# Moving one group of value loads two head pairs later in the source of a fused attention and maxout kernel

## The chip, the cores and the metric

The kernel runs on one core of a Trainium2 chip. The metric is the device time of one execution in microseconds (us). The time before is 335.61 us, the median of five executions that lie between 333.82 and 337.74 us.

## What is computed

The first half is attention with a relative position bias, for 8 batches, 8 heads, 576 positions and 64 values per head; the second is a feed-forward layer with three parallel products and an elementwise maximum. Cut to what matters:

```
scores = q @ k^T / 8 + bias_table[bucket(|i - j|)]      # per batch and head, 576 x 576
attn   = exp(scores - max) / sum(exp(scores - max))
x      = (attn @ v), heads side by side                 # 4608 tokens x 512
h      = maximum(maximum(x @ w1, x @ w2), x @ w3)       # 4608 x 768
out    = h @ w_out                                      # 4608 x 512
```

The inputs are float32; the kernel turns them into bf16 as it loads them, and multiplies in bf16.

## The kernel before

**Batches and head pairs.** After a first batch with a code of its own, one loop runs over batches b = 1 to 7 and, within each, over head pairs hp = 0 to 3 (two heads of 64 fill the 128 partitions). A head pair has two halves. Each half begins with a visit (`visit`): TensorE multiplies kT and qT into PSUM (`sc`), ScalarE takes the exponential (L479) into a tile `e`. VectorE multiplies in the bias band (L473). Then comes an `attend` (tile `a`), the product of such exponentials with the values.

**Late products.** `attend` isn't called at once. Each head pair puts two calls, one per half, in the list `late`, and each half of the loop takes one out (`next_late`). So the values of batch 2 are first read one head pair after batch 2 has begun: batch 2, head pair 0 still multiplies the values of batch 1, head pair 3.

**Feed-forward work as filling.** The products with the weights (`ps`, `pso`) of the batch before are cut into portions, and `fill` puts some of them between the attention products of each half, so that TensorE has work while ScalarE takes exponentials.

**Loads.** `load_q`, `load_k` and `load_v` each issue DMAs from POOL's queue that read float32 from HBM and write bf16 to SBUF. For a whole batch, `load_v` issues four DMAs of 128 KB (as written) into `vx` (L134), one per 128 positions, and two of 32 KB into `vt` (L151) for the last 64 positions: six in all, 576 KB. There are two `vx` and two `vt` buffers; batch b uses number b modulo 2. So batch 2's values overwrite batch 0's, and may be written only when the last `attend` of batch 0 has been done. That one is taken out of `late` in batch 1, head pair 0, second half.

**Crossbar transposes.** The matrix products need q and k with the head dimension on the partitions. For batch 0 and 1, TensorE transposes them. From batch 2 on, DMA transposes do (`transposes`, L415), ten per batch, issued from SP's queue: for each of five groups of positions one for q and one for k. Those of batch 2 are called for in batch 1, one group per half; the generator `crossbar` holds what is left of them. Their sources are the tiles `q_sb` and `k_sb`, which the loads write.

**What sets the order.** Work that is passed through `inorder` (`keep_in_program_order`) stays in the order of the source on its engine. The loads aren't passed through it: the scheduler of the tile framework places them on POOL's queue by their dependences and their place in the source. On the chip each engine then runs its own queue in order, and waits on semaphores for what it needs from others.

**Where the loads of batch 2 and 3 are called.** `load_q` and `load_k` of batch 2 are called in batch 0, last head pair; `load_v` of batch 2 in batch 1, head pair 0, at the end of the second half, after the `attend` and the portions were chosen, as it is for each later batch in the batch before it; `load_q` and `load_k` of batch 3 in batch 1, head pair 3. Between those calls, no other code gives POOL work.

Of the kernel before, what the change touches and what calls it, by code (L numbers as in the profile page):

```python
# [39 lines left out]
def kernel(  # L40
# [13 lines left out]
    B, H, S, D = q.shape  # L54
# [98 lines left out]
    def load_q(b, h0, h1):  # L153
        load_main(q, b, h0, h1, batch[b][0])
        load_tail(q, b, h0, h1, q_diag)

    def load_k(b, h0, h1):
        load_main(k, b, h0, h1, batch[b][1])
        load_tail(k, b, h0, h1, k_diag)

    def load_v(b, h0, h1):
        load_main(v, b, h0, h1, vx[b % 2][:, :, :, 0:D])
        load_tail(v, b, h0, h1, v_diag)
# [14 lines left out]
    def load_tiles():  # L178
        q_sb = loads.tile([P, KT, H, D], BF16, tag="q_sb", name="q_sb")
        k_sb = loads.tile([P, KT, H, D], BF16, tag="k_sb", name="k_sb")  # L180
        return q_sb, k_sb
# [189 lines left out]
    def store_outputs():  # L371

        while stores:
            stores.pop(0)()

    def add_ffn(t0, nt, last=False):
        portions, left = ffn(t0, nt, last)
        portions[0] = rest + portions[0]
        rest[:] = left
        pending.extend((sum(n for n, _ in p), [fn for _, fn in p]) for p in portions)  # L380

    def early():

        if pending and None in pending[0][1]:
            n, fns = pending[0]
            i = fns.index(None)
            for fn in fns[:i]:
                fn()
            pending[0] = (n, fns[i + 1 :])

    def fill(target, *hooks):

        groups, spent, hooks = [], 0, list(hooks)
        while pending and (not groups or spent + pending[0][0] <= target):
            n, fns = pending.pop(0)
            spent += n
            groups += [fn for fn in fns if fn]
        for j, group in enumerate(groups):
            while hooks and (j == len(groups) - 1 or j > 0 and len(hooks) > len(groups) - 1 - j):
                hooks.pop(0)()  # L400
            group()
        for hook in hooks:
            hook()


    def transposes(b):

        made = qk_tiles()
        qk.append(made)

        def one(j, t):
            src = batch[b][j][:, t].rearrange("p h d -> p (h d)") if t < KT else (
                (qtail, ktail)[j][b % 2][:].rearrange("p h c -> p (h c)")
            )
            inorder(nc.sync.dma_start_transpose(out=made[j][:, :, P * t : P * t + P], in_=src))  # L415

        for t in range(KT + 1):
            one(0, t)
            one(1, t)
            yield  # L420
# [37 lines left out]
    def second_transposes(made, hp):  # L458

        hs = slice(2 * hp, 2 * hp + 2)  # L460
        tp = ps_s.tile([P, 2, 2 * CH], BF16, tag="sc", name="tp")
        for j, tl in enumerate((qtail, ktail)):
            for t in range(KT):
                tr(tp[:, j, P * t : P * t + P], batch[1][j][:, t, hs, :].rearrange("p h d -> p (h d)"), ident[:])
            tr(tp[:, j, KT * P : KT * P + P], tl[1][:, hp, :], ident[:])
        for j in range(2):
            dve_copy(made[j][:, hp, :], tp[:, j, 0 : (KT + 1) * P])

    def times_band(hp, e4, t, lo, hi, put=lambda x: x):
        lo, hi = max(lo, P * t - P), min(hi, P * t + 2 * P)  # L470
        if lo < hi:
            c0, c1 = BAND - (hi - P * t + P), BAND - (lo - P * t + P)
            put(nc.vector.tensor_tensor(  # L473
                out=e4[:, t, :, lo:hi], in0=e4[:, t, :, lo:hi],
                in1=hank[:, 2 * hp : 2 * hp + 2, c0:c1][:, :, ::-1], op=ALU.mult,
            ))
# [4 lines left out]
    def visit(qT, kT, e4, c, mid=None):  # L481


        for tt in range(0, KT, 2):
            sc = ps_s.tile([P, 2, 2, QS], F32, tag="sc", name="sc")
            for t in range(2):
                for par in range(2):
                    r = slice(64 * par, 64 * par + 64)
                    mm(
                        sc[:, par, t, :], lhsT=kT[r, P * (tt + t) : P * (tt + t) + P],  # L490
                        rhs=qT[r, c * QS : c * QS + QS],
                    )
            exp(e4[:, tt : tt + 2, :, c * QS : c * QS + QS].rearrange("p t h q -> p h t q"), sc[:])
            if tt == 0 and mid:
                mid()

    def left_keys(hp, qT, kT, el, lo, hi, sc=None):


        if sc is None:  # L500
            sc = ps_s.tile([P, 2 * CH], F32, tag="sc", name="sct")
        for q0 in range(lo, hi, CH):
            q1 = min(q0 + CH, hi)
            mm(sc[:, q0 - lo : q1 - lo], lhsT=kT[:, KT * P :], rhs=qT[:, q0:q1])
        exp(el[:, lo:hi], sc[:, 0 : hi - lo])


    def times_bandt(hp, el):
        inorder(nc.vector.tensor_tensor(
            out=el[:, S - 192 : S + 64], in0=el[:, S - 192 : S + 64], in1=bandt[:, hp, :], op=ALU.mult  # L510
        ))

    def left_queries(hp, qT, kT, el):

        sc = ps_s.tile([P, KT, 2 * 64], F32, tag="sc", name="scq")
        for t in range(KT):
            mm(sc[:, t, :], lhsT=kT[:, P * t : P * t + P], rhs=qT[:, QM : QM + P])
        eq = el[:, S + 64 :].rearrange("p (t h q) -> p t h q", t=KT, h=2)
        exp(eq, sc[:].rearrange("p t (h q) -> p t h q", h=2))
# [68 lines left out]
    def x_tile():  # L588
        return xs.tile([P, KT + 1, d_model], BF16, tag="x_sb", name="x_sb")
# [3 lines left out]
    def next_late():  # L593
        return late.pop(0)() if late else (lambda: None)

    def e_tiles():
        return (
            ep.tile([P, KT, 2, QM], BF16, tag="e4", name="e4"),
            ep.tile([P, S + 64 + KT * P], BF16, tag="el", name="el"),
        )  # L600
# [62 lines left out]
    for hp in range(HP):  # L663
# [18 lines left out]
        def queries():  # L682
            left_queries(hp, qT, kT, el)
            times_band_left(hp, el)
# [28 lines left out]
    for b, hp in [(b, hp) for b in range(1, B) for hp in range(HP)]:  # L713
        if hp == 0:
            x_sb[b] = x_tile()
        qT, kT = (x[:, hp, :] for x in qk[b])
        e4, el = e_tiles()
        rate = 8 if b == 1 or (b, hp) == (2, 0) else 13

        visit(qT, kT, e4, 0)
        store_outputs()
        if b == 1:
            if hp == 0:
                crossbar = transposes(2)
            next(crossbar, None)
        elif hp and b + 1 < B:
            if hp == 1:
                crossbar = transposes(b + 1)  # L730
            next(crossbar)
        early()
        if turned:
            turned.pop(0)()
        quotients = next_late()
        times_band(hp, e4, 0, 0, QS, inorder)
        quotients()
        fill(rate, lambda: left_keys(hp, qT, kT, el, 0, S + 64))
        times_bandt(hp, el)


        visit(qT, kT, e4, 1)
        store_outputs()
        if b == 1 or hp in (1, 2) and b + 1 < B:
            next(crossbar, None)
        early()
        if turned:
            turned.pop(0)()
        quotients = next_late()
        times_band(hp, e4, 1, 0, QM, inorder)  # L750
        quotients()
        if b == 1 and hp + 1 < HP:
            second_transposes(qk[1], hp + 1)
        if hp == 1:
            add_ffn((b - 1) * CH if b > 1 else QS, CH if b > 1 else QS)
        if hp == 0 and b + 1 < B:
            load_v(b + 1, 0, H)
        if hp == (HP - 1 if b == 1 else 0) and b + 2 < B:
            batch[b + 2] = load_tiles()
            load_q(b + 2, 0, H)  # L760
            load_k(b + 2, 0, H)

        def queries():
            left_queries(hp, qT, kT, el)
            times_band(hp, e4, 3, 0, QM, inorder)

        fill(rate, lambda: times_band(hp, e4, 2, 0, QM, inorder), queries)
        times_band_left(hp, el)
        for half in range(2):
            late.append(lambda b=b, hp=hp, e4=e4, el=el, half=half: attend(b, hp, e4, el, half))  # L770
# [44 lines left out]
```

## Time and profile before

| what | value |
|---|---|
| median of five executions | 335.61 us (333.82 to 337.74) |
| the profiled execution | 337.74 us |
| its span, first to last instruction | 336.0 us |
| TensorE (PE) busy | 312.4 us, 93% of the span |
| VectorE (DVE) busy | 212.7 us, 63% |
| ScalarE (ACT) busy | 201.3 us, 60% |
| GpSimd (POOL) busy | 118.4 us, 35%, nearly all of it issuing DMAs |
| moved by DMA | 40.65 MB, 121 GB/s on average |
| mean granted TensorE clock | 0.985 |

The span lies 1.74 us below the time of the same execution. Times in the views are microseconds from the first instruction. "SPq" and "POOLq" are the queues of those engines, where the issue of a DMA takes its time; the landing of the data comes later. A tail in square brackets says how long the engine sat idle before the instruction, and what ended that.

### The profile page before, as it was taken

Reading aid. Unit: us, or ns where it says so; the run is one execution under the profiler, and the core shown is the slowest. Engines: PE = TensorE matmul, PEld = TensorE weight load, DVE = VectorE, ACT = ScalarE, POOL = GpSimd, SP = SyncE. Lnnn points to the kernel's source line nnn. Section 1 sums busy time; section 2 is a strip of 40 time slices with the busy share of each in tenths; the row PEclk is TensorE's granted clock in tenths of the full one; section 3 lists DMA queues with packets and bytes.
Section 4 is the critical chain, followed back from the end, with each engine's and each line's share of the span. In section 5 each row is a group of like instructions: output and inputs, shape, how many; then the busy total and the mean of one; then the engine's idle time right before and its main releaser. Section 6 shows DMA issues by size and latency. Waiting matters only on the chain.

```text
span 336.0 us, 7932 instructions
## 1 busy us (share of the span) xinstructions
PE 312.4 (93%) x3183; PEld 177.2 (53%) x3224; DVE 212.7 (63%) x526; ACT 201.3 (60%) x270; POOL 118.4 (35%) x157
## 2 busy tenths in 40 slices
PE   6878879929999999999999999999999999999995
PEld 2346657717655555555555555555555554444442
DVE  6386667724766676667666766677667666444452
ACT  3699767735877766776677667766776661021221
POOL 8932994609874760294096000410000000000000
PEclk9999999966999999999999999999999999999999
DMA  9999999999999999999999960496022103301103
GB/s 159 150 213 179 99 139 134 121 176 150 141 185 158 150 135 198 137 141 170 234 114 110 174 176 13 58 164 189 19 49 86 64 2 66 132 1 62 64 0 125
DMA packets 171781, 40.65 MB, mean 121 GB/s; under 512 B 163672, under 2 KB 167264, under 8 KB 171744
## 3 DMA queue, kind: packets, MB, share of 16 engines
q0 software_dynamic: 110688, 16.72, 80.2%
q1 hardware_dynamic: 59840, 23.02, 37.2%
q8 instruction: 25, 0.41, 0.5%
q10 hardware_dynamic: 1216, 0.40, 0.5%
q14 instruction: 12, 0.10, 0.1%
HBM read 35.39 MB, written 9.45 MB: 133 GB/s over the span
## 4 chain that ended last, share of the span: by engine, by line
PE 75%; DMA 12%; POOL 8%; issue 2%; SPq 2%; DVE 1%; ACT 0%; POOLq 0%; DVEq 0%
PE ps L94 38%; PE a L94 13%; PE pso L94 12%; PE sc L94 8%; DMA w_bf<-in_moe_w_dram 5%; DMA wo_bf<-in_moe_w_out_dram 3%; PE sct L94 2%; POOL q_sb L134 2%; POOL vx L134 2%; SPq L415 2%; DMA k_sb<-in_k_dram 2%; PE scq L94 2%; DMA kT<-k_sb 2%; POOL k_sb L134 1%; POOL vt L151 1%
## 5 line engine op out<-in xcount | busy, mean ns | idle before, releaser
L94 PE MATMUL ps<-xT,w_bf 128*128 128x512 bf16 (+1 forms) x692 | 154.2, 360 | 1.5
L479 ACT ACTIVATE e<-sc 128x1024 bf16<-128x1024 f32 x128 | 124.9, 1024 | 36.7 <-PE sc L94 36.6
L94 PEld LDWEIGHTS <-w_bf 128*128 128x128 bf16 x720 | 66.4, 99 | 57.6 <-issue 1.7
L473 DVE TENSOR_TENSOR e<-e,hank 128x512 bf16<-128x512 bf16 (+2 forms) x136 | 59.8, 467 | 31.3 <-ACT e L479 29.7
L299 ACT ACTIVATE m<-ps 128x512 bf16<-128x512 f32 x54 | 32.3, 598 | 67.1 <-PE ps L94 64.8
L318 DVE TENSOR_TENSOR m<-ps,m 128x512 bf16<-128x512 f32 x54 | 37.3, 691 | 47.5 <-ACT el L479 27.1
L94 PEld LDWEIGHTS <-kT 64*128 64x128 bf16 (+1 forms) x704 | 36.2, 96 | 47.7 <-issue 27.1
L94 PE MATMUL pso<-wo_bf,hT 128*128 128x512 bf16 x203 | 50.5, 379 | 1.2 <-DVE hT L323 0.5
L94 PE MATMUL sc<-qT,kT 64*128 64x256 bf16 x512 | 42.6, 280 | 9.6 <-DMA kT<-k_sb 4.4
L94 PE MATMUL a<-vx,e 128*128 128x65 bf16 x1024 | 45.5, 194 | 0.0
L134 POOL DMA_DIRECT2D q_sb<-in_q_dram x32 | 28.2, 906 | 38.7 <-DMA kT<-k_sb 25.2
L94 PEld LDWEIGHTS <-e 128*128 128x128 bf16 x1024 | 41.2, 98 | 0.9
L323 DVE TENSOR_TENSOR hT<-ps,m 128x512 bf16<-128x512 f32 x54 | 37.0, 686 | 6.3 <-PE ps L94 4.6
L94 PE MATMUL a<-vt,el 128*128 128x130 bf16 (+1 forms) x192 | 39.9, 214 | 0.9 <-DMA vt<-in_v_dram 0.9
L564 DVE TENSOR_TENSOR x_sb<-a,rd 128x256 bf16<-128x256 f32 (+1 forms) x64 | 31.4, 491 | 2.2
L110 DVE COPY osb<-pso 128x512 f32<-128x512 f32 (+1 forms) x33 | 22.6, 684 | 13.9 <-PE pso L94 10.5
L94 PEld LDWEIGHTS <-hT 128*128 128x128 bf16 x216 | 19.6, 98 | 21.8 <-DVE hT L323 1.5
L94 PEld LDWEIGHTS <-el 128*128 128x128 bf16 x448 | 24.1, 97 | 12.4 <-issue 10.1
L134 POOL DMA_DIRECT2D vx<-in_v_dram x32 | 28.7, 927 | 3.9 <-DMA k_sb<-in_k_dram 1.9
L134 POOL DMA_DIRECT2D k_sb<-in_k_dram x28 | 24.7, 908 | 5.2 <-DMA wo_bf<-in_moe_w_out_dram 4.3
L479 ACT ACTIVATE el<-sct 128x640 bf16<-128x640 f32 (+2 forms) x36 | 23.1, 644 | 3.3 <-PE sct L94 2.6
L479 ACT ACTIVATE el<-scq 128x512 bf16<-128x512 f32 x32 | 19.1, 597 | 8.8 <-PE scq L94 8.7
(61 smaller groups left out, 163.0 us busy)
## 6 DMA issues: line engine op xcount, KB each, us to landing
out_dram<-osb SPq DMA_DIRECT2D x35, 256.0 KB, 2.7
vx<-in_v_dram POOLq DMA_DIRECT2D x32, 128.0 KB, 7.0
q_sb<-in_q_dram POOLq DMA_DIRECT2D x26, 128.0 KB, 5.9
k_sb<-in_k_dram POOLq DMA_DIRECT2D x24, 128.0 KB, 6.2
w_bf<-in_moe_w_dram POOLq DMA_DIRECT2D x3, 768.0 KB, 14.3
xT<-in_k_dram SPq DMA_DIRECT2D x6, 128.0 KB, 4.4
hank<-w_dr SPq DMA_DIRECT2D x2, 384.0 KB, 7.1
wo_bf<-in_moe_w_out_dram POOLq DMA_DIRECT2D x1, 768.0 KB, 10.6
```

Of the source, the lines that this page charges most:

```text
L94: inorder(nc.tensor.matmul(*args, **kw))
L110: inorder(nc.vector.tensor_copy(out_, in_))
L134: nc.gpsimd.dma_start(out=dst[:, t, h0:h1, :], in_=x[:, t, h0:h1, :])
L151: nc.gpsimd.dma_start(out=dst(b, par, h0, h1), in_=tail_part(src, b, h0, h1, par))
L299: nc.scalar.activation(out=st[fb]["m0"][:], in_=st[fb]["ps0"], func=ACTF.Copy)
L318: inorder(nc.vector.tensor_tensor(out=m[:], in0=st[fb]["ps1"], in1=st[fb]["m0"][:], op=ALU.max))
L323: inorder(nc.vector.tensor_tensor(out=hT[:, fb * CH : fb * CH + CH], in0=ps2, in1=st[fb]["m"][:], op=ALU.max))
L415: inorder(nc.sync.dma_start_transpose(out=made[j][:, :, P * t : P * t + P], in_=src))
L473: put(nc.vector.tensor_tensor(out=e4[:, t, :, lo:hi], in0=e4[:, t, :, lo:hi], in1=hank[:, 2 * hp : 2 * hp + 2, c0:c1][:, :, ::-1], op=ALU. ...
L479: nc.scalar.activation(out=out_, in_=in_, func=ACTF.Exp, scale=inv_sqrt_d)
L564: inorder(nc.vector.tensor_tensor(out=x_sb[b][:, 2 * half : 2 * half + n, P * hp : P * hp + P].rearrange("p t (h d) -> p t h d", d=D), in0 ...
```

## The change

The call of `load_v` that stands in batch 1 moves from head pair 0 to head pair 2. It loads the values of batch 2, the third batch. In each later batch the call stays at head pair 0.

```
         if hp == 1:
             add_ffn((b - 1) * CH if b > 1 else QS, CH if b > 1 else QS)
-        if hp == 0 and b + 1 < B:
+        if hp == (2 if b == 1 else 0) and b + 1 < B:
             load_v(b + 1, 0, H)
         if hp == (HP - 1 if b == 1 else 0) and b + 2 < B:
             batch[b + 2] = load_tiles()
             load_q(b + 2, 0, H)
             load_k(b + 2, 0, H)
```

In the source the call stood behind the calls for two of the five groups of batch 2's transposes; it then stands behind all five. It still stands ahead of the loads of batch 3's q and k.

More of the change, by code (lines that the diff above doesn't have):

```diff
@@ L755 @@
             add_ffn((b - 1) * CH if b > 1 else QS, CH if b > 1 else QS)
-        if hp == 0 and b + 1 < B:
+        if hp == (2 if b == 1 else 0) and b + 1 < B:
             load_v(b + 1, 0, H)
```

## The prediction

> **What bounds the kernel now.** I read the page's shares and its chain first, then the waits of TensorE, then the timelines of POOL, SP and TensorE around the change (40 to 90 us), then the order in which the two built programs' instructions stand on each engine.
>
> The page, part 1 and part 4:
>
> ```profile
> PE 312.4 (93%) x3183; PEld 177.2 (53%) x3224; DVE 212.7 (63%) x526; ACT 201.3 (60%) x270; POOL 118.4 (35%) x157
> ...
> PE 75%; DMA 12%; POOL 8%; issue 2%; SPq 2%; DVE 1%; ACT 0%; POOLq 0%; DVEq 0%
> ```
>
> TensorE is busy for 93% of the span, and 75% of the chain that ended last. So a DMA matters only where TensorE waits for it. TensorE's waits between 50 and 110 us are these (engine, line, what it waited for, us in total, times, longest):
>
> ```profile
> PE sc L94 <- DMA kT<-k_sb: 4.4, 3, 2.1
> PE sc L94 <- DMA qT<-q_sb: 1.7, 1, 1.7
> PE sct L94 <- ACT e L479: 0.2, 1, 0.2
> ```
>
> No row has the values (`vx`, `vt`) as its cause; the first two are the transposes. They fall at one place, the beginning of batch 2. TensorE's timeline there (start, us, instruction, count, idle before):
>
> ```profile
> 59.05 0.22 PE L97 MATMUL tp<-ident,ktail 128*128 128x128 bf16 x1
> ...
> 69.31 0.28 PE L94 MATMUL sc<-qT,kT 64*128 64x256 bf16 x2 [1.68 <-DMA qT<-q_sb]
> 70.82 0.39 PE L94 MATMUL sc<-qT,kT 64*128 64x256 bf16 x2 [1.23 <-DMA kT<-k_sb]
> 72.27 0.40 PE L94 MATMUL sc<-qT,kT 64*128 64x256 bf16 x2 [1.05 <-DMA kT<-k_sb]
> 74.77 0.40 PE L94 MATMUL sc<-qT,kT 64*128 64x256 bf16 x2 [2.10 <-DMA kT<-k_sb]
> ...
> 83.78 0.41 PE L94 MATMUL a<-vx,e 128*128 128x65 bf16 x8
> ```
>
> The four holes are 1.68 + 1.23 + 1.05 + 2.10 = 6.06 us. The first row is the last instruction of the transposes by TensorE that the source calls in batch 1, head pair 2 (`second_transposes`); I use it below as a clock for the place in the source. The last row is the first product with batch 2's values: visit and `attend` in batch 2, head pair 1. Batch 2, head pair 0 multiplies batch 1's (its `attend`s are those at 75.18 and 81.07).
>
> POOL's timeline shows when the moved loads are really issued:
>
> ```profile
> 55.69 2.64 POOL L134 DMA_DIRECT2D k_sb<-in_k_dram  x3 [4.29 <-DMA wo_bf<-in_moe_w_out_dram]
> 58.30 1.33 POOL L151 DMA_DIRECT2D ktail<-in_k_dram  x2
> 59.62 3.54 POOL L134 DMA_DIRECT2D vx<-in_v_dram  x4
> 63.73 1.26 POOL L151 DMA_DIRECT2D vt<-in_v_dram  x2 [0.58 <-DMA k_sb<-in_k_dram]
> 74.82 3.53 POOL L134 DMA_DIRECT2D q_sb<-in_q_dram  x4 [9.83 <-issue]
> ```
>
> **The change, part by part.** It removes no instruction and adds none; it moves six DMA issues in the source. What matters is where they stood on POOL's queue, and what they waited for.
>
> *What the old place was worth.* The old call stands behind the last `attend` of batch 0, whose products TensorE finishes at about 41.7 us (the row `a<-vx,el` at 41.55, four products, 0.28 us). If POOL had been free, the values could have been issued then. They were issued at 59.62, 17.9 us later, because twelve loads of q and k of batch 2 stand ahead of them, the last of which ends at 58.30 + 1.33 = 59.63. POOL went from that row to the values without a gap. So nothing in the old place decided their time: POOL's queue did.
>
> *What the new place asks for.* It stands behind batch 1, head pair 2's `second_transposes`, whose last instruction starts at 59.05 on TensorE, 0.57 us ahead of 59.62. Even if the scheduler tied the loads to the place in the source, TensorE's order would ask POOL to wait for nothing: it would be past that place. But POOL has no such tie. It waits on semaphores alone: for a free DMA lane and for TensorE's last reading of the buffer (at 41.7 us), neither of which the move touches.
>
> *Which queue neighbours they pass.* None. Between the two places the source gives POOL nothing else to do: ahead of the six stand the q and k loads called in batch 0, and behind them those of batch 3, called in head pair 3. On SP, the transposes and the stores stay where they are, since they are another queue's. The built programs say the same. In both, POOL's rows around the six are (row, line, instruction, semaphores waited for):
>
> ```
> 60 L151 DMACopy ktail_99<-in_k_dram 64x4x64 [waits DMASW3_49]
> 61 L151 DMACopy ktail_99<-in_k_dram 64x4x64 [waits DMASW4_49]
> 62 L134 DMACopy vx_93<-in_v_dram 128x8x64 [waits DMASW5_49,PE_49]
> ...
> 67 L151 DMACopy vt_95<-in_v_dram 64x4x64 [waits DMASW2_49]
> 68 L134 DMACopy q_sb<-in_q_dram 128x8x64 [waits DMAHW5_49,DMAHW3_49,DMAHW7_49,DMAHW1_49,DMASW3_49]
> ```
>
> All 160 rows of POOL and 139 of SP are the same. On TensorE, VectorE and ScalarE the rows differ in the serial numbers within tiles' names (`ps_875` becomes `ps_869`: six loads fewer were named ahead of it), and in nothing else. With those numbers left out, the two programs agree in every instruction, buffer address, semaphore and waited-for value. The move is visible in the source and not on the chip.
>
> *The sum.* Issue of the six: 4 x 0.9 + 2 x 0.64 = 4.9 us before (rows of 3.54 us for four and 1.26 us for two), 4.9 us after, at the same place: 0. TensorE's holes before batch 2: 6.06 us before and after: 0. Waits added: none, so nothing is queued behind one. The cover of the loads stays too: the last `vt` issue starts at about 64.4 and its kind lands within 7.6 us (the range in this window is 7.3 to 7.6), so at 72.0; first need at 83.7, that is 11.7 us to spare. There is no cost that the trace leaves unknown, hence nothing to bound. The profiled execution stays at 337.74 + 0 = 337.74 us (336.0 span and 1.74 outside it). That execution is the slowest of the five, 2.13 us above their median, and nothing in the change prefers it, so the forecast for the median is **335.6 us**.
>
> The Trainium skill has a rule against such a move: "DMA: Bandwidth & Descriptors", section "Rules for kernel authors", tells authors to issue a DMA early and wait late, so that its fixed cost is overlapped. By it a later issue loses cover, and the sum would be above 335.6. The rows decide: the issue is at 59.62 by the queue, whichever place the source names.
>
> **The rivals.**
>
> *Faster: the loads do move behind the transposes.* The transposes of batch 2 run from 56.33 (first issue on SP) to 74.7, and the loads are issued among them; in the stretches from 60 to 75 us DMA moves 113, 157 and 159 GB/s. The six write 4 x 128 + 2 x 32 = 576 KB, 0.59 MB; at 157 GB/s that is 3.8 us of DMA time, by which the last transpose could land earlier. That is the low end. The high end is the whole stall of 6.06 us and the slow clock behind it: the granted clock is 0.55 in 70 to 75 us and 0.50 in 75 to 80 us, and the work from 75.09 to 81.01 (5.92 us) takes 3.27 us where it stands at 62.14 to 65.41. So 6.06 + 2.65 = 8.7 us. The time would be 335.6 - 3.8 = 331.8 (nearest row: the shared traffic), down to 326.9. For it: the stall is real and the loads do overlap the transposes. Against it: POOL issues them at 59.62 in either program, in the middle of the transposes. Chance 0.02.
>
> The Trainium skill bears on this, in the same page, section "Issuing engines are not separate DMA queues": DMAs from different issuing engines run on the same engines and interleave, so values on POOL's queue can slow transposes on SP's. That would make the gain above plausible if the loads moved; no row here separates the two streams.
>
> *Slower: the loads are held until the transposes have landed.* This needs one wait on POOL ahead of row 62, for the transposes. The last hole closes at 74.72; then 5.4 us for the issue train (59.62 to 64.99) and 7.6 us for the last landing give 87.7. The first product with the values is at 83.7, so TensorE waits 4.0 us, and the slow clock behind such a hole (2.65 us above) may come on top: +4.0 to +6.7, 339.6 to 342.3; I take 339.6, since the clock dip has one example. It decides from the point at which the train starts later than 83.7 - 5.4 - 7.6 = 70.7 us. The loads of batch 3's q and k, next on POOL at 74.82, would be 5.4 us later too. For it: the words of the change say "behind". Against it: row 62 waits for a DMA lane and for TensorE, and for none of SP's transposes. Chance 0.02.
>
> By the Trainium skill's fit in that page (section "Anatomy of one DMA — SWDGE (gpsimd) path", about 2.0 us plus the bytes at 436 GB/s), 128 KB would land in an estimated 2.3 us; this trace has 6.6 to 8.5 us for these loads, so the measured landing is used.
>
> *No difference: the same program twice.* Chance 0.96. What remains is the scatter of executions.
>
> **How the numbers follow.** The likeliest case gives 335.6. Its range is the scatter of one program: the five executions before lie between 333.82 and 337.74, so 333.8 to 337.7. The rivals hold 0.04 together and are left out, which the 2 in 10 allow. One per cent is 3.4 us, about what a measurement of this kernel can tell from no change, and near the whole spread of five executions (3.9 us). Faster by over 1%: the faster rival's 0.02; slower: 0.02; within 1%: 0.96.
>
> **What would show it right or wrong.** In the changed kernel's profile the first `vx` load of batch 2 should follow the last `ktail` load without a gap, near 59.6 us, with SP's transposes from 56 to 74 us around it; TensorE should still wait some 6 us in four holes before batch 2, with a granted clock near one half behind them; and the busy times should repeat within tenths of a microsecond for PE. The forecast is wrong if the `vx` loads start behind 70 us, if the holes are shorter by 3.8 us or more, or if a new wait for `vx` or `vt` stands near 83.7 us. A shift of the median by 1 to 2 us with the same rows would be scatter, not the change.

## The result

The changed kernel takes 334.99 us (median of 43 executions), the kernel before 335.07 us (80 executions). The ratio is 1.0007, with a 95% interval of 0.9995 to 1.002 (it is not the quotient of the two medians, which is 0.9998). The forecast was 335.6 us and "no difference". Executions of the kernel before spread from 332.38 to 337.74 us. In what follows each kernel is compared with executions of the kernel before on the same chip; their medians were 334.15 to 335.0 us.

The profiled execution of the changed kernel has a span of 334.1 us, 1.9 us less than the one before. Parts 1 and 4 of its page:

```profile
PE 311.6 (93%) x3183; PEld 177.3 (53%) x3224; DVE 212.7 (64%) x526; ACT 201.2 (60%) x270; POOL 118.5 (35%) x157
...
PE 70%; DMA 16%; POOL 7%; issue 2%; ACT 2%; DVE 1%; SPq 1%; POOLq 0%; DVEq 0%; ACTq 0%
```

The instruction counts are the same as before, and the busy times within 0.1 us, but for TensorE's 0.8. POOL's timeline around the moved loads (start, us, instruction, count, idle before):

```profile
56.99 0.62 POOL L151 DMA_DIRECT2D ktail<-in_k_dram  x1 [0.15 <-DMA qtail<-in_q_dram]
57.60 3.54 POOL L134 DMA_DIRECT2D vx<-in_v_dram  x4
61.09 1.29 POOL L151 DMA_DIRECT2D vt<-in_v_dram  x2
72.52 3.52 POOL L134 DMA_DIRECT2D q_sb<-in_q_dram  x4 [10.14 <-issue]
76.01 3.53 POOL L134 DMA_DIRECT2D k_sb<-in_k_dram  x4
```

The last load of k ends at 56.99 + 0.62 = 57.61, and the values follow without a gap, as before the change. They start 2.0 us earlier than in the profile of before, not later: POOL's wait for w_out (`wo_bf`) ahead of the k loads was 2.59 us in this execution and 4.29 in that one. On the chip the two programs are the same; these are differences between two executions. TensorE's timeline at the beginning of batch 2:

```profile
69.04 0.28 PE L94 MATMUL sc<-qT,kT 64*128 64x256 bf16 x2 [1.74 <-DMA kT<-k_sb]
69.92 0.28 PE L94 MATMUL sc<-qT,kT 64*128 64x256 bf16 x2 [0.59 <-DMA kT<-k_sb]
72.40 0.39 PE L94 MATMUL sc<-qT,kT 64*128 64x256 bf16 x2 [2.20 <-DMA kT<-k_sb]
...
81.15 0.41 PE L94 MATMUL a<-vx,e 128*128 128x65 bf16 x8
```

Three holes, 1.74 + 0.59 + 2.20 = 4.53 us, where the profile of before had 6.06 in four. The first product with batch 2's values (the last row) waits for nothing.

### The profile page after: what moved, and what is told of

Read it like the earlier page. It is cut to its first block, busy times and chain, and to the rows that moved or that the text cites. A ratio compares the mean times of both kernels' runs of the same rounds, so it can differ in the third digit from the quotient of the medians.

```text
span 334.1 us, 7932 instructions
## 1 busy us (share of the span) xinstructions
PE 311.6 (93%) x3183; PEld 177.3 (53%) x3224; DVE 212.7 (64%) x526; ACT 201.2 (60%) x270; POOL 118.5 (35%) x157
## 4 chain that ended last, share of the span: by engine, by line
PE 70%; DMA 16%; POOL 7%; issue 2%; ACT 2%; DVE 1%; SPq 1%; POOLq 0%; DVEq 0%; ACTq 0%
PE ps L94 35%; PE pso L94 12%; PE a L94 11%; PE sc L94 7%; DMA w_bf<-in_moe_w_dram 5%; DMA vt<-in_v_dram 3%; DMA k_sb<-in_k_dram 3%; DMA kT<-ktail 2%; DMA q_sb<-in_q_dram 2%; PE sct L94 2%; POOL q_sb L134 2%; POOL vx L134 2%; DMA kT<-k_sb 1%; PE scq L94 1%; POOL k_sb L134 1%
## 5 line engine op out<-in xcount | busy, mean ns | idle before, releaser
L94 PEld LDWEIGHTS <-w_bf 128*128 128x128 bf16 x720 | 66.4, 99 | 57.6 <-issue 1.7
L94 PE MATMUL a<-vx,e 128*128 128x65 bf16 x1024 | 46.4, 195 | 0.0
L94 PEld LDWEIGHTS <-e 128*128 128x128 bf16 x1024 | 42.1, 99 | 1.0 <-issue 0.2
```

What stands on the lines that cost most here:

```text
L94: inorder(nc.tensor.matmul(*args, **kw))
```

## The experiments

The theory was that the move does nothing because POOL's queue, and not the place in the source, decides when the loads are issued. That leaves three questions. What would a real move have done? How far must the call go before POOL's order changes? And what sets TensorE's holes before batch 2, which the values' traffic was said to stretch?

### The values held until the transposes have landed

```
-        if hp == 0 and b + 1 < B:
-            load_v(b + 1, 0, H)
+        if hp == (2 if b == 1 else 0) and b + 1 < B:
+            hold(b); load_v(b + 1, 0, H)
...
+    def hold(b): b == 1 and (held.append(1), [inorder(nc.gpsimd.tensor_copy(gate[:], m[:, 0, 0 : 5 * P : P])) for m in qk[2]])
```

`put` passes the next eighteen loads (batch 2's values, then batch 3's q and k) through `inorder`, so that they stay behind the two copies.

> POOL waits for all ten transposes of batch 2 before it issues the six loads of values (two small copies on POOL read qT and kT), so the move that the source describes is made real. By my price the first vx load starts at about 74 us instead of 59, lands at about 87, and TensorE waits some 4 us for vx or vt ahead of its first product with batch 2's values; the loads' share of 0 to 3.8 us comes off the holes before batch 2. Net 0 to +4.0 us, 335.1 to 339.1, and up to 341.8 if the clock slows behind the new hole as well. The faster rival expects a gain: 331.3 or less, no wait for the values. The changed kernel's own theory (no tie between POOL and the source's place) expects this kernel alone, and not the change, to move the vx row in POOL's timeline.

Measured: 342.32 us, 1.0202 of the kernel before (1.0168 to 1.0236), +5.6 to +7.9 us. POOL's timeline:

```profile
72.09 0.19 POOL L165 COPY gate<-kT 128x5 bf16<-128x5 bf16 x1
72.61 3.52 POOL L134 DMA_DIRECT2D vx<-in_v_dram  x4 [0.32 <-issue]
```

TensorE's rows that sat idle before, from batch 2 on:

```profile
70.13 0.28 PE L94 MATMUL sc<-qT,kT 64*128 64x256 bf16 x2 [2.75 <-DMA kT<-k_sb]
81.16 0.28 PE L94 MATMUL a<-vt,el 128*128 128x130 bf16 x1 [3.12 <-DMA vt<-in_v_dram]
110.21 0.39 PE L94 MATMUL sc<-qT,kT 64*128 64x256 bf16 x2 [3.65 <-DMA kT<-k_sb]
```

So this is what "behind the transposes" looks like when it is real: the loads start at 72.6 and not at 57.6. The holes before batch 2 shrink to 2.75 us, a new one of 3.12 us opens for the values (I had 4.0), and a third of 3.65 us opens before batch 3, since its loads and with them its transposes are late. Together 9.52 us of holes, against 4.53 and 6.06. With the rest of the 6.8 us goes a lower mean clock, 0.969 here and 0.984 in the changed kernel.

Not all of batch 3's delay comes from the wait for the transposes. Its q starts 4.8 us later than in the changed kernel, about as much as the six loads ahead of it take; its k, which follows q directly there (72.52 and 76.01), starts 9.4 us later:

```profile
77.31 3.58 POOL L134 DMA_DIRECT2D q_sb<-in_q_dram  x4
85.39 1.88 POOL L134 DMA_DIRECT2D k_sb<-in_k_dram  x2 [0.51 <-DMA q_sb<-in_q_dram]
```

Between the two stand other loads, an order that this kernel's edit brought with it. So a part of the third hole, and of the 6.8 us, is this kernel's own, and how large it is no run shows. My prediction had named the delay of batch 3's loads and priced it at nothing.

### One step further in the source

```
-        if hp == 0 and b + 1 < B:
+        if hp == 0 and 1 < b < B - 1:
             load_v(b + 1, 0, H)
...
             load_q(b + 2, 0, H)
             load_k(b + 2, 0, H)
+            if b == 1:
+                load_v(b + 1, 0, H)
```

> The call of load_v for batch 2 stands behind the loads of batch 3's q and k, one head pair later than in the change. In the built program the four vx loads keep their place on POOL's queue and the two vt loads go behind eight loads of batch 3, which wait for the transposes. If POOL's order decides, vx starts near 59 us as before and vt near 82, landing near 90, so TensorE waits some 6 to 7 us for vt ahead of its first product with batch 2's values: +6 to +9.5 us, 341 to 345. If the source's place had some effect of its own, vx would start later too. If the loads were hidden anyway: no change.

Measured: 340.92 us, 1.0179 (1.0152 to 1.0205), +5.1 to +6.9 us, at the low end of what was expected. POOL's timeline:

```profile
56.32 3.53 POOL L134 DMA_DIRECT2D vx<-in_v_dram  x4
70.77 3.50 POOL L134 DMA_DIRECT2D q_sb<-in_q_dram  x4 [10.92 <-issue]
74.23 3.53 POOL L134 DMA_DIRECT2D k_sb<-in_k_dram  x4
77.70 1.32 POOL L151 DMA_DIRECT2D vt<-in_v_dram  x2
```

and TensorE's hole:

```profile
84.78 0.29 PE L94 MATMUL a<-vt,el 128*128 128x130 bf16 x1 [6.18 <-DMA vt<-in_v_dram]
```

The same call, moved past other loads, costs 6.0 us through two loads of 32 KB. The four `vx` loads went as far in the source and did not move on the queue (they start at the end of the last load of k, at 56.32); no wait for them appears. POOL's order decides.

### Batch 2's values left out

```
-        if hp == 0 and b + 1 < B:
+        if hp == 0 and 1 < b < B - 1:
             load_v(b + 1, 0, H)
```

> This kernel leaves out the six loads of batch 2's values (batch 2 is multiplied with what batch 0 left in the buffers), so it shows the most that moving them away from the transposes could give. If the values' traffic delays the transposes of batch 2 by its own share (the faster rival's low end), TensorE's four holes before batch 2 shrink by 3.8 us or more and the time is 331.3 us or less against a median of 335.1 before; with the slow clock behind the holes gone too, down to 326.4. If q and k's own loads set those holes, the holes stay at 4.5 to 6.1 us and the time within 1 us of 335.1. In both, everything behind batch 2 is as before.

Measured: 335.07 us, 1.0003 (0.9971 to 1.0035). No gain can be told from noise when the values are taken away altogether. TensorE's holes:

```profile
69.01 0.28 PE L94 MATMUL sc<-qT,kT 64*128 64x256 bf16 x2 [2.49 <-DMA kT<-k_sb]
74.38 0.71 PE L94 MATMUL sct<-qT,kT 128*128 128x512 bf16 x2 [3.51 <-DMA kT<-ktail]
```

6.00 us, but the larger hole has another cause: `sct`, the first product that needs the tails' transposes, which are the last two. In this kernel POOL went on to batch 3's loads at 66.48, into the gap that the values had left. So I repeated it with POOL held at that point as well:

```
-        if hp == 0 and b + 1 < B:
-            load_v(b + 1, 0, H)
+        if hp == (2 if b == 1 else 0) and b + 1 < B:
+            load_v(b + 1, 0, H) if b > 1 else hold(b)
```

Here `put` keeps only the next four loads, batch 3's q, behind the copies.

> As the kernel without batch 2's values (they are left out here too), but POOL also waits for all ten transposes of batch 2 before it goes on to batch 3's q and k (all but one k load), so that nothing on POOL's queue follows into the gap. If shared traffic with whatever POOL loads next is what stretches the transposes, TensorE's holes before batch 2 shrink to some 2.7 us (as in the kernel with the values held) from 4.5 to 6.2, and the time falls by 1.8 to 3.5 us plus up to 2.6 for the clock: 329 to 333.3 against 335.0. If the gap was not refilled but is set by SP's own issue train, the holes stay at 4.5 to 6.2 us and the time within 1 us of 335.0.

Measured: 333.70 us, 0.9996 (0.9976 to 1.0017). The expectation of a gain fell. The holes, with no load on POOL's queue from 57.5 to 70.3 us:

```profile
69.71 0.28 PE L94 MATMUL sc<-qT,kT 64*128 64x256 bf16 x2 [2.48 <-DMA kT<-k_sb]
73.76 0.45 PE L94 MATMUL sct<-qT,kT 128*128 128x512 bf16 x2 [2.19 <-DMA kT<-ktail]
```

4.67 us: inside what two executions of the kernel with the values show. The second hole is a wait for the last transpose, which takes 3.8 us to land; two loads of batch 3's k go out beside it, at 70.30 and 71.73. In the kernel with the values held only one load of 32 KB goes out at that time (71.39), the last transpose lands in 2.4 us, and TensorE doesn't wait for it: 2.75 us of holes. So this kernel doesn't show all that a quiet queue gives. The transposes themselves do gain. From issue to landing (minimum, median, maximum in us, of the instructions of L415 between 52 and 74 us), first in the changed kernel, then in this one:

```profile
DMA to landing us min/median/max: 3.3/6.6/8.3
```

```profile
DMA to landing us min/median/max: 2.4/4.1/6.1
```

But SP issues them one after another, and that train hardly changes. Its first and last row in the changed kernel:

```profile
54.29 1.29 SPq L415 DMA_TRANSPOSE qT<-q_sb  x1
...
70.02 1.87 SPq L415 DMA_TRANSPOSE kT<-ktail  x1
```

and without the values, and POOL held:

```profile
54.02 1.29 SPq L415 DMA_TRANSPOSE qT<-q_sb  x1
...
69.94 1.21 SPq L415 DMA_TRANSPOSE kT<-ktail  x1
```

From the first issue to the end of the last it is 71.89 - 54.29 = 17.6 us in the one and 71.15 - 54.02 = 17.1 us in the other. Less traffic brings the transposes home 2.5 us sooner in the median, and takes 0.5 us off the train at whose end the last one stands.

### Feeding that train earlier, and turning it round

In the profiles of the two kernels SP waits 2.4 us after the first transpose for the first tile of k, and POOL waits for w_out, 4.29 us before and 2.59 after. Three kernels change what is loaded when; three more change the order of the train.

```
-    nc.gpsimd.dma_start(out=wo_bf[:], in_=moe_w_out.rearrange("(c p) m -> p c m", p=P))
+    for c in range(0, FCH, 3): nc.gpsimd.dma_start(out=wo_bf[:, c : c + 3, :], in_=moe_w_out.rearrange("(c p) m -> p c m", p=P)[:, c : c + 3, :])
```

> The load of w_out (768 KB) is issued as two of 384 KB, with the values' call as before. In the profiles POOL sits idle for 2.6 to 4.3 us ahead of batch 2's k loads, waiting for w_out to land. If that wait is what makes batch 2's q and k late, it shrinks to 1 or 2 us at the price of one more issue (0.9 us), the k loads start 1 to 3 us earlier, TensorE's holes before batch 2 shrink by as much, and the time is 332 to 334.5. If the DMA engines are full there and the wait costs nothing, the holes stay at 4.5 to 6.1 us and the time within 1 us of 335.1.

Measured: 334.36 us, 0.9983 (0.9962 to 1.0003). POOL's wait for w_out fell to 0.78 us, the holes to 0.62 + 1.46 + 2.06 = 4.14 us. The time lies in both of the ranges expected, and by itself it can't be told from no change.

```
-                load_q(2, 0, H)
-                load_k(2, 0, H)
+                for t in range(KT): load_main(q, 2, 0, H, batch[2][0], t, t + 1); load_main(k, 2, 0, H, batch[2][1], t, t + 1)
+                load_tail(q, 2, 0, H, q_diag); load_tail(k, 2, 0, H, k_diag)
```

> The loads of batch 2's q and k are interleaved by position group (q0 k0 q1 k1 ...) and not q first, then k. In the profiles SP issues batch 2's first transpose (q) and then waits 2.3 to 2.4 us for the first k tile; the other nine follow at some 1.3 to 1.5 us each. If that train sets the holes, its second issue comes 2 to 2.4 us earlier, the last transpose lands as much earlier, the holes shrink by 2 us or more and the time is 331 to 333.5. If the DMA engines' traffic sets them, the holes stay at 4.5 to 6.1 us and the time within 1 us of 335.0.

Measured: 336.34 us, 1.0069 (1.0052 to 1.0086): slower, where a gain was expected. Against the changed kernel's profile the train ran earlier (its second issue at 54.94 and not at 58.07) and ended 2.7 us earlier, at 69.21. But its transposes took a median of 8.3 us to land, and TensorE's holes grew to 6.42 us:

```profile
68.96 0.28 PE L94 MATMUL sc<-qT,kT 64*128 64x256 bf16 x2 [2.08 <-DMA kT<-k_sb]
73.58 0.39 PE L94 MATMUL sc<-qT,kT 64*128 64x256 bf16 x2 [4.34 <-DMA kT<-k_sb]
```

That the earlier transposes run against the loads of k that are still under way would explain the longer landing, but no run here separates the two.

> As the interleaved kernel, and the load of w_out in two halves. If POOL's wait for w_out still counts once q and k are interleaved, another 0.5 to 1.5 us: 330 to 332.5; if not, as the interleaved kernel within 1 us.

Measured: 336.06 us, 1.005 (1.0024 to 1.0076): as the interleaved kernel (the two intervals overlap).

The other edit, in `transposes`:

```
-        for t in range(KT + 1):
-            one(0, t)
-            one(1, t)
+        for (i, t), (j, u) in (((0, 0), (1, 0)), ((0, 1), (1, 1)), ((1, 2), (1, 3)), ((0, 2), (0, 3)), ((0, 4), (1, 4))):
+            one(i, t)
+            one(j, u)
             yield
```

> As the interleaved kernel, and the crossbar transposes of every batch in the order q0 k0, q1 k1, k2 k3, q2 q3, tails, so that what the first visit reads (k0 to k3, q0, q1) is complete after six transposes and not eight. Two transposes of some 1.3 us earlier: the holes before the first visit's products shrink by a further 2 us; the product for the left keys, which needs all ten, then waits instead where the filling does not cover it. 329.5 to 332 if it is covered, as the interleaved kernel within 1 us if not.

Measured: 334.18 us, 1.0009 (0.9987 to 1.0031). The order gave back what the interleaving had lost; the gain to 332 us or less that was expected of it did not come. Without the interleaving:

> The changed kernel with its loads as they are, and the crossbar transposes of every batch in the order q0 k0, q1 k1, k2 k3, q2 q3, tails. Against the interleaved kernel this order took the time from 1.0069 to 1.0009 of the kernel before. If its worth is the same without the interleaving, the time is 0.994 of the kernel before, 332.1 us at a median of 334.2. If it only made good what the interleaving lost, the time is within 0.3% of the kernel before.

Measured: 332.24 us, 0.9946 (0.9918 to 0.9974): the order keeps its worth without the interleaving. TensorE waits 0.51 us for the transposes before batch 2, and then 1.06 us for ScalarE:

```profile
68.14 0.28 PE L94 MATMUL sc<-qT,kT 64*128 64x256 bf16 x2 [0.51 <-DMA kT<-k_sb]
69.48 0.80 PE L94 MATMUL sc<-qT,kT 64*128 64x256 bf16 x4 [1.06 <-ACT e L479]
```

And with w_out in two halves:

> The same order of transposes, and w_out loaded in two halves, with the values' call at its old place (which gives the same instructions as the new one). The halves gave 0.9983 (0.9962 to 1.0003) by themselves; if both are real and add up, 0.992, some 331.5 us; if neither is, within 0.3% of the kernel before.

Measured: 331.16 us, 0.9919 (0.9896 to 0.9943), 2.7 us less than the kernel before; the intervals of the two overlap, so the halves' own part stays unproven. TensorE's holes:

```profile
67.25 0.28 PE L94 MATMUL sc<-qT,kT 64*128 64x256 bf16 x2 [0.27 <-DMA kT<-k_sb]
68.30 0.62 PE L94 MATMUL sc<-qT,kT 64*128 64x256 bf16 x4 [0.77 <-DMA kT<-k_sb]
72.05 0.45 PE L94 MATMUL sct<-qT,kT 128*128 128x512 bf16 x2 [1.55 <-DMA kT<-ktail]
```

The values are where they always were, and the holes are 2.59 us. This version is faster than the kernel before, and so than the changed one, which is the same program.

## Why the prediction was right, and where its parts were not

**The move is not visible on the chip: right.** The values follow the last load of k without a gap, at 57.60 us here, and the two executions differ as executions of one program do. The further step in the source shows why: `vx` stayed, `vt` went behind eight other loads, and only `vt` made TensorE wait.

**The sum of 0: right.** Measured 1.0007 (0.9995 to 1.002). The forecast of 335.6 us took the median of five executions; the median of eighty is 335.07. (The row `a<-vx,el` of the prediction ends at 41.55 + 0.28 = 41.83 us and not at 41.7, which changes nothing.)

**What the profile was to show: in part.** The holes before batch 2 were "some 6 us in four" and are 4.53 us in three. The granted clock behind them is 0.59 in 70 to 75 us and 0.73 in 75 to 80, where I had near one half, and TensorE's busy time differs by 0.8 us and not by tenths. I had taken one execution's holes for the program's; in POOL's wait for w_out alone the two differ by 1.7 us.

**The faster rival's price: too high.** The step that failed is "576 KB at 157 GB/s, by which the last transpose could land earlier", 3.8 us at the least. Without the values, and with no load on POOL's queue until 70.3 us, the time is 0.9996 (0.9976 to 1.0017) of before: a gain of 0.8 us at the most. The traffic is shared, as the Trainium skill says of DMAs from different engines ("DMA: Bandwidth & Descriptors", section "Issuing engines are not separate DMA queues"), and these runs show it: 6.6 us to landing with the values, 4.1 without. But the last transpose waits for its turn in SP's train of 17 us, and TensorE's first products wait for where k stands in it: the order of the train alone gave 0.9946. A bandwidth was priced where an issue order counts as well.

That the order is all isn't shown. With the values held, and one load beside the last transpose, the holes before batch 2 were 2.75 us, 1.8 and 3.3 us less than in the two profiles with the values; what that kernel lost later hides what this is worth in time. And with q and k interleaved the train ended 2.7 us earlier, and the holes grew to 6.42 us. How much belongs to the order and how much to the landing stays open.

**The slower rival's price: one term left out.** Its own hole was 4.0 us in the prediction and 3.12 in the run. Its "loads of batch 3's q and k would be 5.4 us later too" was left without a price. In the run q came 4.8 us later and k 9.4 us, in part by that kernel's own order of loads, and a hole of 3.65 us followed. In all +6.8 us (5.6 to 7.9), where I had taken +4.0 and had +6.7 as the upper end.

**The rule against a later issue.** The same page's section "Rules for kernel authors" tells authors to issue a DMA early. It did not apply to this change, in which the issue stayed put; the two kernels in which the issue is really later, at 72.6 and 77.7 us, are slower by 6.8 us (in part by its own order of loads) and 6.0 us, as the rule would have it.

## What to carry to other kernels

A call that issues DMAs has a place in the source and a place on its queue. Read the second: look up when the queue reaches the instruction, what stands ahead of it, and whether any neighbour is passed; a move between places where the queue holds nothing else was no change here. Before pricing a wait for a chain of transfers by its bytes, look at how the chain is issued: here its order was worth 0.5%, and leaving out 576 KB beside it gained nothing that could be told from noise.

## What the runs showed of the hardware

- Taking 576 KB away from beside ten crossbar transposes cut their median time from issue to landing from 6.6 to 4.1 us, and the time of SP's issue train only from 17.6 to 17.1 us: one transpose holds SP for 1.2 to 1.95 us with the traffic and for 1.2 to 2.4 us without.
- The granted clock fell behind TensorE's holes, but neither their sum nor the longest of them settles by how much. In stretches of 5 us (PE, PEld, DVE, ACT and POOL busy with their counts, then the granted clock, the DMA share and GB/s), first the changed kernel, with holes of 4.53 us:

```profile
70.00:75.00 5.00, 2.80 (x28) 2.08 (x29) 1.03 (x3) 1.42 (x2) 2.48 (x3) 0.59 1.09 170
75.00:80.00 5.00, 5.00 (x58) 3.53 (x57) 2.24 (x5) 2.43 (x3) 5.00 (x7) 0.73 2.05 133
```

  the kernel with the other order of transposes, with holes of 0.51 and 1.06 us:

```profile
70.00:75.00 5.00, 4.96 (x46) 3.31 (x44) 1.69 (x4) 1.79 (x3) 2.12 (x3) 0.67 1.24 193
```

  and the one with that order and w_out in two halves, with holes of 2.59 us in three pieces:

```profile
70.00:75.00 5.00, 3.45 (x55) 2.52 (x54) 2.10 (x5) 1.97 (x3) 3.29 (x4) 1.00 1.06 209
```

  In the last the clock stays at 1.00, from 75 to 80 us too. The Trainium skill ("TensorE: Matmul & The Clock Gate", section "HAM oscillation — how this bites in real kernels") warns of idle gaps above some 3.4 us. In the changed kernel no single hole is above 2.20 us, and it still falls; with the other order of transposes two holes of at most 1.06 us went ahead of a fall to 0.67, while 2.59 us of holes went ahead of none. What decides between them was not settled.
- Interleaving the loads of q and k, by which the second transpose of batch 2 started 3.1 us earlier and their train ended 2.7 us earlier, made the kernel 0.7% slower, with landings of 8.3 us (median). Why they are so slow was not settled.
